# Another sequence of the same operations: linear attention and an MLP-mixer on one core

## The chip, the cores and the metric

The kernel runs on one core of a Trainium2 chip. The metric is the device time of one execution in microseconds (us). Five engines have queues of their own: TensorE (PE, matmuls), VectorE (DVE), ScalarE (ACT), GpSimd (POOL) and SyncE (SP, which here issues loads and stores). Each engine takes its instructions strictly in order, and an instruction waits on semaphores for what other engines or transfers must have done.

## The reference

Two blocks, joined by a reshape. The first is a recurrence over the sequence for each of 4 batches and 8 heads (48 wide, 768 steps); the second is an MLP-mixer on the result, first over tokens, then over channels.

```python
B, H, S, D = 4, 8, 768, 48
for t in range(S):
    cur = np.einsum('bhd,bhe->bhde', u[None] * k[t], v[t])
    y[t] = np.einsum('bhd,bhde->bhe', r[t], state + cur)
    state = w[t][:, :, :, None] * state + np.einsum('bhd,bhe->bhde', k[t], v[t])
x = y.transpose(0, 2, 1, 3).reshape(B, S, H * D)
h = np.maximum(x.transpose(0, 2, 1) @ w_tok1, 0) @ w_tok2
z = x + h.transpose(0, 2, 1)
out = z + np.maximum(z @ w_ch1, 0) @ w_ch2
```

w_tok1 is 768x256, w_tok2 256x768, w_ch1 384x1536, w_ch2 1536x384.

## The kernel before

**Attention units.** A batch's 768 tokens are three units of 256, so there are 12 units, 0 to 11 (batch = unit // 3). A unit has 4 chunks of 64 tokens. Its pieces carry names, and the change speaks only of these names; `0.gram` is the piece gram of unit 0. In the ORDER of the later units they are written 3/gram.

- DVE: ends (the scan of the decay w from the end of each chunk, line 435), begins (the scan from its start, line 443), keys and queries (k and r multiplied by these, lines 440 and 446), put and mask (products from PSUM into the matrix of a chunk, lines 458 and 327).
- ACT: own0 to own3 (k times u, line 331), copied0 and copied1 (turned keys out of PSUM, line 350), by1 to by3 (the state times the decay of a chunk, line 501; by0 for the first chunk of a later unit), seen (line 389 or 392), taken0 to taken2 (the output into x, line 407), and the range checks small and large (line 427), which only set a flag that is read at the kernel's end.
- PE: own (k times u against r, line 315), tokens (keys turned, line 345), gram (k against r, line 315), carry (k against v for the state, line 365), up1 to up3 (the state's step, line 508; in units 3 to 11 on DVE), before (r against the states, line 380) and after (the chunk's matrix against v, line 401).
- Loads on SP: k, r, v and w of a unit (k0 is k of unit 0; rk3 is both of unit 3 in four transfers). Lines 188, 201, 181.

Units 0 to 2 have rooms of their own; from unit 3 on k and r use two buffers in turn. For unit 0 to 2, own, gram and before take turns in two PSUM buffers, so each waits until what was made two pieces before has been read out.

**Weights.** The weights come as 64-bit words and are turned on chip into 32-bit floats, in chunks of 1024 columns: t0 to t2 for the token weights, c0 to c8 for the channel weights. A chunk has the steps load (SP, line 261), plus and minus (ACT, lines 264 and 267), lead, two, value and sum (DVE, lines 270, 273, 277, 281). The `sum` of the ORDER's chunks is called put there.

**Mixer.** Batch 0 is computed with plain 32-bit matmuls: h0 to h11 (line 947; h[2c + i] is token chunk c and half i), relu0 and relu1 of the two halves (line 950), back0 to back5 (line 958, with an add on DVE, line 960), turn (x turned, line 969, with a copy on ACT, line 971), up (line 993, or 989 in its last third) and down (line 1004). Batches 1 to 3 split each factor into two or three rounded parts and use three passes of a faster matmul: hidden (667), back (726), turn (741), ends and joint (772, 774, 779; the up-projection, with POOL and DVE forming its parts in lines 754 to 765), down (790 to 792). The third parts of the weights lie in DRAM and come through a ring of 10 slots (line 626). The attention of batch b + 1 is worked in between the mixer's matmuls of batch b.

**What sets the order.** Two lists written into the source. The first part (units 0 to 2, token weights, c0, the h pieces and back0) is one call of `strict` with the pieces in their order (lines 1094 to 1109). The rest (1181 pieces) is put together by `interleaved` from nine streams: each digit of ORDER names the stream whose next piece follows (0 the mixer, 1 to 3 and 8 its side streams and the weights, 4 to 6 the units modulo 3, 7 the loads of units). `strict` chains all instructions of an engine in the order of the list:

```python
for ins in block.instructions[done:]:
    if ins.engine in in_turn:
        if in_turn[ins.engine]:
            tc.add_manual_dep(ins, in_turn[ins.engine], no_sync, reason="order of issue")
        in_turn[ins.engine] = ins.name
```

This holds for PE, DVE, ACT and SP. `behind(gate, f)` in addition holds the first instruction of f until the piece `gate` has ended; it is used for loads. The six PSUM banks of the later stage are handed out in the order of the list too.

## Time and profile before

| | us |
|---|---|
| runs | 477.54, 477.70, 480.27 (median 477.7) |
| the profiled execution | 478.31 |
| its span | 476.5 |

| engine | busy us | share of the span | instructions |
|---|---|---|---|
| PE | 459.1 | 96% | 5322 |
| DVE | 344.6 | 72% | 495 |
| ACT | 265.8 | 56% | 606 |
| POOL | 54.2 | 11% | 58 |

Loads and stores moved 85.34 MB, 179 GB/s on average over the span. A row of a timeline reads: start, duration, engine, line, operation, output<-inputs, how many instructions are merged in it, and in brackets how long the engine stood before it and what released it. A row of the waits reads: who, line, whom it waited for, total us, how often, the longest. A row by windows reads: the stretch, its length, busy us (and instructions) of PE, of its weight loads, of DVE, ACT and POOL, then the granted clock, the busy share of the transfer engines and GB/s.

### The profile page before, as it was taken

How to read it: one execution, taken by the hardware profiler on the slowest of the kernel's cores; microseconds unless marked ns; L12 is line 12 of the kernel's file. 1: busy time of each engine (PE TensorE's matmuls, PEld its weight loads, DVE VectorE, ACT ScalarE, POOL GpSimd, SP SyncE). 2: the span in 40 equal slices, each digit the busy share in tenths (PEclk: the TensorE clock that was granted, in tenths of full speed). 3: DMA queues.
4: the chain of work that ended last, by engine and by line, in shares of the span. 5: the costliest groups of instructions: out<-in, count | busy, mean ns of one | idle time of the engine just before them, and what ended most of it. 6: DMA issues, size and time to landing. Idle time of an engine off the chain costs nothing.

```text
span 476.5 us, 12778 instructions
## 1 busy us (share of the span) xinstructions
PE 459.1 (96%) x5322; PEld 409.6 (86%) x5322; DVE 344.6 (72%) x495; ACT 265.8 (56%) x606; POOL 54.2 (11%) x58
## 2 busy tenths in 40 slices
PE   3899999999999999999999999999999999999996
PEld 2776588856797668999999999999999999999995
DVE  7998797679598877876897998685587885235341
ACT  6699876674678856453747385351837554134140
POOL 1000000000000001231302002130304003032130
PEclk9999999999999999999999999999999999999999
DMA  8865745573584556963888842754784513336331
GB/s 313 317 221 217 188 169 191 180 275 99 152 228 138 177 179 207 284 186 100 252 283 232 294 154 56 198 173 141 215 227 150 167 61 84 115 101 199 86 99 54
DMA packets 45055, 85.34 MB, mean 179 GB/s; under 512 B 4736, under 2 KB 37376, under 8 KB 44992
## 3 DMA queue, kind: packets, MB, share of 16 engines
q1 hardware_dynamic: 44704, 84.37, 56.3%
q8 instruction: 43, 0.70, 0.6%
q14 instruction: 20, 0.16, 0.1%
q10 hardware_dynamic: 288, 0.10, 0.1%
HBM read 72.65 MB, written 11.80 MB: 177 GB/s over the span
## 4 chain that ended last, share of the span: by engine, by line
PE 90%; ACT 4%; DVE 2%; DMA 2%; issue 1%; SPq 0%; DVEq 0%; ACTq 0%
PE bank L1004 10%; PE bank L772 8%; PE bank L779 8%; PE bank L774 8%; PE bank L790 8%; PE bank L792 8%; PE bank L791 8%; PE bank L993 7%; PE bank L667 3%; PE bank L989 3%; PE bank L726 3%; PE bank L315 2%; PE bank L401 2%; PE bank L380 2%; PE kv_ps L365 2%; PE bank L669 2%
## 5 line engine op out<-in xcount | busy, mean ns | idle before, releaser
L765 POOL TENSOR_TENSOR z_high<-z_high 128x384 fp32r<-128x384 f32 x48 | 52.9, 1107 | 406.7 <-DMA ring<-third 186.8
L754 ACT ACTIVATE z_high<-bank 128x384 fp32r<-128x384 f32 x48 | 23.5, 489 | 58.1 <-PE bank L779 57.7
L772 PE MATMUL bank<-x_forms,forms 128*128 128x384 f32 x216 | 50.3, 341 | 0.0
L779 PE MATMUL bank<-z_more,forms 128*128 128x384 f32 x216 | 50.1, 340 | 0.0
L774 PE MATMUL bank<-x_forms,ring 128*128 128x384 f32 x216 | 49.3, 337 | 0.0
L761 DVE SCALAR_TENSOR_TENSOR z_high<-bank,z_high 128x384 fp32r<-128x384 f32 x48 | 26.5, 554 | 31.4 <-ACT z_high L754 29.4
L1004 PE MATMUL bank<-wch,z 128*128 128x384 f32 x144 | 48.1, 488 | 0.0
L790 PE MATMUL bank<-forms,z_high 128*128 128x384 f32 x140 | 47.8, 342 | 0.0
L792 PE MATMUL bank<-forms,z_high 128*128 128x384 f32 x140 | 47.1, 337 | 0.0
L791 PE MATMUL bank<-ring,z_high 128*128 128x384 f32 x140 | 47.1, 337 | 0.0
L798 DVE SCALAR_TENSOR_TENSOR x<-bank,x 128x384 f32<-128x384 f32 x35 | 18.8, 553 | 39.0 <-PE bank L792 38.9
L1004 PEld LDWEIGHTS bank<-wch,z 128*128 128x128 f32 x144 | 26.8, 190 | 17.2
L501 ACT ACTIVATE before<-state,to_end 112x48 f32<-112x48 f32 x132 | 33.1, 324 | 13.0 <-DVE state L516 7.6
L779 PEld LDWEIGHTS bank<-z_more,forms 128*128 128x128 f32 x216 | 39.0, 188 | 0.1
L772 PEld LDWEIGHTS bank<-x_forms,forms 128*128 128x128 f32 x216 | 38.3, 188 | 0.5
L774 PEld LDWEIGHTS bank<-x_forms,ring 128*128 128x128 f32 x216 | 38.6, 188 | 0.0
L993 PE MATMUL bank<-xT,wch 128*128 128x256 f32 x144 | 32.0, 381 | 0.0
L993 PEld LDWEIGHTS bank<-xT,wch 128*128 128x128 f32 x144 | 27.0, 190 | 3.7
L757 ACT ACTIVATE z_high<-z_high 128x384 fp32r<-128x384 f32 x48 | 25.2, 525 | 3.5
L790 PEld LDWEIGHTS bank<-forms,z_high 128*128 128x128 f32 x140 | 26.3, 188 | 0.2
L791 PEld LDWEIGHTS bank<-ring,z_high 128*128 128x128 f32 x140 | 26.3, 188 | 0.0
L792 PEld LDWEIGHTS bank<-forms,z_high 128*128 128x128 f32 x140 | 26.3, 188 | 0.0
(243 smaller groups left out, 961.2 us busy)
## 6 DMA issues: line engine op xcount, KB each, us to landing
ring<-third SPq DMA_DIRECT2D x144, 192.0 KB, 3.4
raw<-in_words_ch_dram SPq DMA_DIRECT2D x8, 1023.8 KB, 4.8
rk<-in_rk_dram SPq DMA_DIRECT2D x36, 192.0 KB, 5.2
near<-in_near_dram SPq DMA_DIRECT2D x8, 768.0 KB, 5.0
w<-in_w_dram SPq DMA_DIRECT2D x10, 520.5 KB, 5.1
vt<-in_v_dram SPq DMA_DIRECT2D x12, 384.0 KB, 5.0
out_dram<-x SPq DMA_DIRECT2D x17, 192.0 KB, 2.8
third<-forms SPq DMA_DIRECT2D x12, 192.0 KB, 3.3
```

The costliest lines, as they stand in the source:

```text
L501: act.mul(t[:ROWS, a], state[bt, g][:ROWS, a], by_last(c, j)[:, a:a + 1])
L757: act.mul(z_form(jt, 2), z_form(jt, 0).bitcast(f32), 1.0 / BASE)
L761: dve.scalar_tensor_tensor(z_form(jt, 1), a, 0.0, z_form(jt, 0).bitcast(f32), op0=ALU.max, op1=ALU.subtract)
L765: pool.tensor_add(z_form(jt, 2), z_form(jt, 2).bitcast(f32), z_form(jt, 1).bitcast(f32))
L772: pe.matmul(a, up[m], xf(0)[:, m], start=m == 0, stop=False)
L774: pe.matmul(a, low[:, m], xf(1)[:, m], start=False, stop=False)
L779: pe.matmul(banks["a", jt], joint, xf(2)[:, m], start=False, stop=m == 2)
L790: pe.matmul(a, z[0], up, start=first, stop=False, skip_group_check=True)
L791: pe.matmul(a, z[1], held[bt, s, half, 1, jt], start=False, stop=False, skip_group_check=True)
L792: pe.matmul(a, z[2], joint, start=False, stop=last, skip_group_check=True)
L993: pe.matmul(ps, now["wch1"][:, jt // 4, m, ts(jt % 4, 128)], xT[:, m, ts(s, SEG)], start=(m == 0), stop=(m == DM // 128 - 1))
L1004: pe.matmul(ps, zs[s][:, jt, ts(n, 128)], now["wch2"][:, jt, :], start=(jt == 0), stop=(jt == NJ - 1))
```

## The change

No operation is added, removed or resized. The list of the first part is now a string of names, FIRST, in another order; ORDER has other digits. What a name stands for is as before; `a<b` holds a until b has ended, with the same gates as before. The two range checks of a unit are now two names, small and large.

```diff
--- before.py
+++ after.py
@@ -48,17 +48,28 @@
 SHRINK = (1.0 - 1.0 / BASE) ** 2
 LEAST, MOST = 2.0 ** -40, 2.0 ** 40
 MID = 3 * G // 4 * SEG1
+FIRST = (
+    "k0 masks 0.own0 0.own1 0.ends 0.own2 0.begins 0.own3 r0 0.large v0 k1 0.own 1.own0 1.own1 0.keys w1 0.queries 0.put 1.ends 1.own2 "
+    "0.tokens 1.own3 1.keys 0.copied0 1.begins 0.gram 0.mask r1 0.copied1 w2 0.small 0.carry 0.up0 0.by1 0.up1 0.by2 0.up2 0.by3 2.ends "
+    "t0.load<0.tokens 1.tokens t0.plus 1.copied0 1.copied1 1.own 1.queries 0.before 0.seen k2<1.ends 2.own0 v1<0.by2 2.own1 0.up3 1.by0 "
+    "0.after 1.put 1.carry 1.up0 2.own2 2.own3 r2<0.tokens 0.taken1 t0.minus 2.own 1.by1 1.up1 2.keys 2.tokens 0.taken0 t0.lead t0.two 1.by2 "
+    "1.up2 0.taken2 2.put 1.gram t1.load 1.by3 v2 t2.load<1.by1 1.up3 t0.value t0.sum 1.before 2.copied1 h1 2.copied0 1.mask t1.minus h3 "
+    "2.by0 2.carry 2.up0 1.seen 1.after 2.begins t1.plus 2.by1 2.up1 h0 1.taken1 2.queries 2.gram 1.taken0 2.by2 2.up2 1.taken2 h2 t1.lead "
+    "h5 2.by3 t2.plus 2.before h7 2.seen t1.two t2.minus 2.mask 2.after h4 2.taken0 2.taken1 t1.value t1.sum c0.load<1.gram h6 t2.lead "
+    "t2.two t2.value t2.sum 2.taken2 h8 c0.plus h9 c0.minus c0.lead c0.two h10 h11 relu1 c0.value relu0 back0 c1.load<2.own c2.load<1.tokens "
+    "1.large v3 rk3 w3<2.by3 2.large 1.small 2.small"
+)
 ORDER = (
-    "888008088078808800000888484440800840804080880808804844088488400448088408008888080080884808884040488844488888084840880880"
...
+    "408880880008088800008888444404008888888880000008880000848844444088808048488844400888880000880888884447444888444000888000"
...
 )
 
 
@@ -533,7 +544,7 @@
         def each(f, n):
             return [lambda m=m: f(m) for m in range(n)]
 
-        return dict(ranges=each(ranges, 2), ends=ends, keys=keys, begins=begins, queries=queries, own_u=each(own_u, A),
+        return dict(small=lambda: ranges(0), large=lambda: ranges(1), ends=ends, keys=keys, begins=begins, queries=queries, own_u=each(own_u, A),
                     own_gram=own_gram, copied=each(copied, UC), taken=each(taken, 3),
                     own_put=own_put, products=[lambda n=n: products(n) for n in range(3)], sums_put=sums_put,
                     tokens=tokens, gram=gram, mask=mask, carry=carry, before=before, seen=seen, after=after,
@@ -1037,7 +1048,7 @@
         loads = piece(lambda: load_rk(i + 1), "loads", ("Q", 8.0, last("before", "gram", "tokens")))
         ends = piece(e["ends"], "ends", ("DVE", 2.6, last("small", "large", "by3", "w")))
         keys = piece(e["keys"], "keys", ("DVE", 1.25, k("ends") + last("loads")))
-        small, large = (piece(e["ranges"][n], name, ("ACT", 1.4, k("ends"))) for n, name in enumerate(("small", "large")))
+        small, large = (piece(e[name], name, ("ACT", 1.4, k("ends"))) for name in ("small", "large"))
         begins = piece(e["begins"], "begins", ("DVE", 2.35, k("ends")))
         tokens = piece(e["tokens"], "tokens", ("PE", 0.9, k("keys") + last("carry"), "k0", "k1"))
         copied = [piece(e["copied"][n], f"copied{n}", ("ACT", 0.6, k("tokens")), ("free", f"k{n}")) for n in range(2)]
@@ -1085,28 +1096,24 @@
     raw_words.append(turned["xT"].rearrange("p m t -> p (m t)").bitcast(u32)[:, :4 * PIECE])
     to_tok = conversion(("wtok1", "wtok2"), words_tok, rooms=lambda n: ((0, 1, 3)[n], n % 2))
     to_ch = conversion(("wch1", "wch2"), words_ch, rooms=lambda n: (n % 2, n % 2) if n else (2, 2))
-    e0, e1, e2 = (unit(i) for i in range(UB))
-    (_, p0, n0, lead0, two0, put0, add0), (_, p1, n1, lead1, two1, put1, add1), (_, p2, n2, lead2, two2, put2, add2) = to_tok
-    _, p3, n3, lead3, two3, put3, _ = to_ch[0]
+    first = {i: unit(i) for i in range(UB)}
     in_turn.update({pe.engine: None, dve.engine: None, act.engine: None, sp.engine: None})
-    s0, s1, s2 = (e["updates"] for e in (e0, e1, e2))
-    t0, t1, t2 = (e["scaled"] for e in (e0, e1, e2))
-    strict(lambda: load_part(0, 1), masks, e0["ends"], e0["own_u"][0], e0["own_u"][1], e0["own_u"][2], e0["own_u"][3], e0["begins"],
-           lambda: load_part(0, 0), e0["keys"], lambda: load_part(1, 1), e0["own_gram"], lambda: load_v(0), e0["ranges"][0], lambda: load_w(1),
-           e0["tokens"], e0["queries"], e1["own_u"][0], e1["own_u"][1], e0["copied"][0], lambda: load_w(2), e0["gram"], e1["ends"], e0["copied"][1],
-           lambda: load_part(1, 0), e0["carry"], e1["own_u"][2], s0[0], e0["own_put"], e1["own_u"][3], e0["ranges"][1], t0[1], s0[1],
-           behind(e0["tokens"], to_tok[0][0]), e1["begins"], behind(e1["ends"], lambda: load_part(2, 1)), e1["own_gram"], t0[2], e1["keys"],
-           e2["own_u"][0], s0[2], e2["own_u"][1], e1["own_put"], t0[3], e1["tokens"], behind(e0["tokens"], lambda: load_part(2, 0)),
-           e0["before"], e2["own_u"][2], e0["mask"], e1["copied"][0], p0, e0["seen"], s0[3], e2["own_u"][3], behind(t0[2], lambda: load_v(1)),
-           e2["ends"], e1["copied"][1], t1[0], e0["after"], e0["taken"][0], e1["carry"], n0, to_tok[1][0], s1[0], e1["queries"], e0["taken"][1],
-           e2["keys"], lead0, t1[1], e2["own_gram"], two0, s1[1], e0["taken"][2], e2["own_put"], e2["tokens"], t1[2], put0, e2["copied"][0],
-           s1[2], t1[3], e2["copied"][1], e1["gram"], s1[3], e1["before"], t2[0], p1, add0, lambda: load_v(2), e1["mask"], e2["carry"], e1["seen"],
-           h[1], s2[0], h[0], e2["ranges"][0], e2["begins"], behind(t1[1], to_tok[2][0]), t2[1], n1, h[3], e2["queries"], s2[1], lead1, two1,
-           e1["after"], t2[2], s2[2], put1, e2["gram"], behind(e1["gram"], to_ch[0][0]), h[2], e1["taken"][0], e1["taken"][1], t2[3], e1["taken"][2],
-           behind(t2[3], lambda: load_w(3)), p2, add1, e2["mask"], lambda: load_v(UB), behind(e2["own_gram"], to_ch[1][0]), e2["before"], h[4],
-           e2["seen"], n2, e2["after"], lead2, two2, h[5], e2["taken"][0], h[6], e2["taken"][1], put2, e2["taken"][2], h[7], h[8], p3,
-           h[10], add2, n3, behind(e1["tokens"], to_ch[2][0]), lead3, two3, rectified[0], h[9], h[11], rectified[1], e1["ranges"][0], e2["ranges"][1], e1["ranges"][1],
-           lambda: load_rk(3), put3, lambda: turned["back"](0))
+    named = {"masks": masks, "rk3": lambda: load_rk(3), "back0": lambda: turned["back"](0)}
+    named.update({f"h{n}": f for n, f in enumerate(h)})
+    named.update({f"relu{n}": f for n, f in enumerate(rectified)})
+    for kind, weights in (("t", to_tok), ("c", to_ch[:3])):
+        for n, steps in enumerate(weights):
+            named.update({f"{kind}{n}.{name}": f for name, f in zip(("load", "plus", "minus", "lead", "two", "value", "sum"), steps)})
+    for i, e in first.items():
+        named.update({f"{'rk'[n]}{i}": lambda i=i, n=n: load_part(i, n) for n in range(2)})
+        named.update({f"w{i + 1}": lambda i=i: load_w(i + 1), f"v{i}": lambda i=i: load_v(i)})
+        for name, made in e.items():
+            name = {"own_u": "own", "own_gram": "own", "own_put": "put", "scaled": "by", "updates": "up"}.get(name, name)
+            named.update({f"{i}.{name}{n}": f for n, f in enumerate(made)} if isinstance(made, list) else {f"{i}.{name}": made})
+    named["v3"] = lambda: load_v(UB)
+    for name in FIRST.split():
+        name, _, gate = name.partition("<")
+        strict(behind(named[gate], named[name]) if gate else named[name])
 
     six_banks.close()
     ps_g, ps_m = None, six_banks.enter_context(tc.tile_pool(name="ps_m", bufs=1, space=bass.MemoryType.PSUM))
```

The old list of the first part and the new one, by engine and in the same names:

```
PE  old: 0.own 0.tokens 0.gram 0.carry 0.up0 0.up1 1.own 0.up2 1.tokens 0.before 0.up3 0.after 1.carry 1.up0 2.own 1.up1 2.tokens 1.up2 1.gram 1.up3 1.before 2.carry h1 2.up0 h0 h3 2.up1 1.after 2.up2 2.gram h2 2.before h4 2.after h5 h6 h7 h8 h10 h9 h11 back0
PE  new: 0.own 0.tokens 0.gram 0.carry 0.up0 0.up1 0.up2 1.tokens 1.own 0.before 0.up3 0.after 1.carry 1.up0 2.own 1.up1 2.tokens 1.up2 1.gram 1.up3 1.before h1 h3 2.carry 2.up0 1.after 2.up1 h0 2.gram 2.up2 h2 h5 2.before h7 2.after h4 h6 h8 h9 h10 h11 back0
ACT old: masks 0.own0 0.own1 0.own2 0.own3 0.small 1.own0 1.own1 0.copied0 0.copied1 1.own2 1.own3 0.large 0.by1 0.by2 2.own0 2.own1 0.by3 2.own2 1.copied0 t0.plus 0.seen 2.own3 1.copied1 1.by0 0.taken0 t0.minus 0.taken1 1.by1 0.taken2 1.by2 2.copied0 1.by3 2.copied1 2.by0 t1.plus 1.seen 2.small 2.by1 t1.minus 2.by2 1.taken0 1.taken1 2.by3 1.taken2 t2.plus 2.seen t2.minus 2.taken0 2.taken1 2.taken2 c0.plus c0.minus relu0 relu1 1.small 2.large 1.large
ACT new: masks 0.own0 0.own1 0.own2 0.own3 0.large 1.own0 1.own1 1.own2 1.own3 0.copied0 0.copied1 0.small 0.by1 0.by2 0.by3 t0.plus 1.copied0 1.copied1 0.seen 2.own0 2.own1 1.by0 2.own2 2.own3 0.taken1 t0.minus 1.by1 0.taken0 1.by2 0.taken2 1.by3 2.copied1 2.copied0 t1.minus 2.by0 1.seen t1.plus 2.by1 1.taken1 1.taken0 2.by2 1.taken2 2.by3 t2.plus 2.seen t2.minus 2.taken0 2.taken1 2.taken2 c0.plus c0.minus relu1 relu0 1.large 2.large 1.small 2.small
DVE old: 0.ends 0.begins 0.keys 0.queries 1.ends 0.put 1.begins 1.keys 1.put 0.mask 2.ends 1.queries 2.keys t0.lead t0.two 2.put t0.value t0.sum 1.mask 2.begins 2.queries t1.lead t1.two t1.value t1.sum 2.mask t2.lead t2.two t2.value t2.sum c0.lead c0.two c0.value
DVE new: 0.ends 0.begins 0.keys 0.queries 0.put 1.ends 1.keys 1.begins 0.mask 2.ends 1.queries 1.put 2.keys t0.lead t0.two 2.put t0.value t0.sum 1.mask 2.begins 2.queries t1.lead t1.two 2.mask t1.value t1.sum t2.lead t2.two t2.value t2.sum c0.lead c0.two c0.value
SP  old: k0 r0 k1 v0 w1 w2 r1 t0 k2 r2 v1 t1 v2 t2 c0 w3 v3 c1 c2 rk3
SP  new: k0 r0 v0 k1 w1 r1 w2 t0 k2 v1 r2 t1 v2 t2 c0 c1 c2 v3 rk3 w3
```

The ORDER's beginning, decoded: on ACT the old one starts with c1.plus c1.minus turn0 turn1 c2.plus c2.minus turn2 turn3 3/own0 to 3/own3, the new one with 3/own0 c1.plus c1.minus turn0 turn1 c2.plus turn2 turn3 c2.minus 3/own1 to 3/own3. On DVE the old one starts with c0.put back1 back2 c1.lead c1.two c1.value back3 c1.put back4 back5, the new one with back1 c0.put back2 c1.lead c1.two back3 c1.value back4 c1.put back5 (these back pieces are the adds of line 960). The loads of unit 4's k and r came first and now come behind the load of c8.

On PE the order of the mixer's own matmuls stays nearly as it was. The units' pieces stand between them in runs, each of them here in brackets with nothing else between:

```
old: [3/tokens] [3/own] [3/carry 3/gram] [4/tokens] [3/before 4/carry 4/gram 3/after] [5/tokens] [4/before 5/carry 5/gram 4/after] [5/before] [5/after] [6/tokens] [6/carry 6/gram] [7/tokens] [7/carry 6/before] [6/after 7/gram] [8/tokens] [7/before 8/carry] [8/gram 7/after] [8/before 8/after] [9/tokens] [9/carry 9/gram] [10/tokens] [9/before] [9/after 10/carry 10/gram] [11/tokens] [10/before] [11/carry 11/gram 10/after] [11/before 11/after]
new: [3/tokens 3/own] [3/carry 3/gram] [3/before] [4/tokens 3/after] [4/carry 4/gram] [4/before] [5/tokens] [5/carry 5/gram 4/after] [5/before] [5/after] [6/tokens] [6/carry] [6/gram] [6/before] [7/tokens 6/after] [7/carry 7/gram] [7/before] [8/tokens] [8/carry] [7/after 8/gram] [8/before] [8/after] [9/tokens] [9/carry 9/gram] [9/before] [10/tokens 9/after] [10/carry 10/gram] [11/tokens 10/before] [11/carry] [11/gram 10/after] [11/before 11/after]
```

More of the change, by code (lines that the diff above doesn't have):

```diff
@@ new lines @@
+FIRST = (
[9 rows of a table added]
+)
+ORDER = (
+    "408880880008088800008888444404008888888880000008880000848844444088808048488844400888880000880888884447444888444000888000"
+    "844000888888845500000008800008488588888440855885585544888800054808805555545558800700555558558888688500000008855050006666"
+    "666600888860088888876656688660066880666556099858886666888000066066666908988000990444444448800088444000884801110884440008"
+    "404428000000000000000000000000000202244440000700004444450000002204470000000050000000002000550005545500005452220004010100"
+    "155520555500000005550002455555000050500000000000000005500066600607066666060600566666666000006566660000006600000400000000"
+    "116660114100500001004400000222020516049916111166991110122110004432443322993442334444000070000010001100000444000000000000"
+    "000000000400044444000004555000000000000004005000000000000004440005054555050000000000145501000555510044005000070050000000"
+    "000555000055500055000000600660000000665500660000066600000000000000600000065566166616060000005611666616600102025562026669"
+    "111116660099010111122101032339922933000230000000001110000000000000000000000000000000000000000000000000000000000000000000"
+    "00000000000000010110000000000000000000000000000000000000700000000000000000000000000000000000000000000"
```

9 lines of the change are left out of this document (removed).

## The prediction

> **What bounds the kernel now.** I read the page's busy shares first, then the stretches by window, then the waits of TensorE.
>
> ```profile
> PE 459.1 (96%) x5322; PEld 409.6 (86%) x5322; DVE 344.6 (72%) x495; ACT 265.8 (56%) x606; POOL 54.2 (11%) x58
> ...
> 0.00:12.00 12.00, 3.71 (x76) 3.30 (x78) 9.01 (x14) 7.50 (x16) 1.26 (x10) 1.00 0.86 314
> 60.00:72.00 12.00, 12.00 (x62) 10.61 (x61) 11.72 (x15) 8.47 (x17) 0.00 (x0) 1.00 0.46 172
> 456.00:476.50 20.50, 15.79 (x91) 15.47 (x89) 6.16 (x12) 4.04 (x8) 3.91 (x4) 1.00 0.14 46
> ...
> PE gram L315 <- DMA rk<-in_rk_dram: 7.6, 1, 7.6
> PE kv_ps L508 <- ACT before L501: 1.4, 3, 1.0
> PE k_ps L345 <- issue: 0.7, 1, 0.7
> PE bank L969 <- ACT raw L267: 0.6, 1, 0.6
> PE bank L401 <- ACT seen L392: 0.6, 2, 0.3
> PE h_ps L947 <- issue: 0.5, 1, 0.5
> PE bank L401 <- issue: 0.5, 1, 0.5
> ```
>
> TensorE is busy 459.1 of 476.5 us. Of its 17.4 idle us, 7.6 are the wait for the first r rows, and 4.7 lie behind its last matmul (20.50 less 15.79); no reordering inside reaches either. The other waits in these rows, with the 0.42 in a row below, sum to 4.7. So the kernel has two stages: up to 60 us TensorE waits for ACT, DVE and the loads; from 60 us on its queue is full, and there a new sequence can only change what the switch from one kind of matmul to another costs, or open a new wait.
>
> **The start-up, to 24 us.** TensorE's rows, with one of ACT:
>
> ```profile
> 16.20 0.98 PE L508 MATMUL kv_ps<-before,ident 112*112 112x192 f32 x2 [0.99 <-ACT before L501]
> 17.11 1.99 PE L315 MATMUL gram<-rk,near 48*64 48x64 f32 x64
> 23.01 0.58 PE L508 MATMUL kv_ps<-before,ident 112*112 112x192 f32 x2
> 24.01 1.15 PE L401 MATMUL y_ps<-vt,at 64*64 64x48 f32 x64 [0.42 <-ACT seen L389]
> 30.53 1.16 PE L315 MATMUL gram<-rk 48*64 48x64 f32 x64
> ...
> 17.21 0.87 ACT L501 ACTIVATE before<-kv_ps,first 112x48 f32<-112x48 f32 x4 [1.07 <-PE kv_ps L508]
> ```
>
> Before, 0.up1 (16.20) is followed by 1.own (17.11), and 0.by2, which needs 0.up1, runs on ACT meanwhile (17.21). In the new order 0.up2 comes straight behind 0.up1 and needs that 0.by2: TensorE stands from about 17.2 to 18.1, 1.0 us. The same five pieces (up1, up2, 1.tokens, 1.own, 0.before) follow in either order, so 0.before ends 1.0 later. It is given back at 24.01: there 0.after waited for 0.seen, which stood on ACT behind t0.plus; now t0.plus follows 0.by3 at once: 0.up2 ends at 19.1, 0.by3 (0.87) at 20.1, t0.plus (1.2, the rows of ACT below) at 21.3, before 0.seen can run. I take 0; the ends are -0.5 (all of the wait and a little more) and +1.0 (nothing is given back). The new SP order (v0 ahead of k1, r1 ahead of w2, v1 ahead of r2) delays k1, w2 and r2 by one transfer each. I cost it at nothing, since TensorE's pieces at half rate from 10 to 16 us hide it; without that cover a transfer of 0.5 MB at the 314 GB/s of the first window is 1.7 us.
>
> The rows also show a clock that opens late: 64 matmuls of L315 take 1.99 us at 17.11 and 1.16 at 30.53, a pair of L508 0.98 at 16.20 and 0.58 at 23.01. The opening came about 6.8 us (23.01 less 16.20) after TensorE's last wait. The new last wait ends at 18.1. One row can't tell a delay after a wait from a fixed time, so the forecast moves nothing here, and rival 3 holds both ways.
>
> [...]
>
> **From 24 us to the first up-projection.** Rows of TensorE, ACT and DVE, two of DVE's at 38.59 and 41.00 for a rival:
>
> ```profile
> 43.62 1.24 PE L947 MATMUL h_ps<-x,wtok 128*128 128x384 f32 x3
> 45.38 3.81 PE L947 MATMUL h_ps<-x,wtok 128*128 128x384 f32 x11 [0.53 <-issue]
> 49.04 1.66 PE L958 MATMUL kv_ps<-h,wtok 128*128 128x384 f32 x4
> 59.08 3.19 PE L993 MATMUL bank<-xT,wch 128*128 128x256 f32 x14
> ...
> 6.12 1.70 ACT L331 ACTIVATE near<-rk,u_col 112x256 f32<-112x256 f32 x4 [1.54 <-DMA rk<-in_rk_dram]
> 43.76 1.45 ACT L407 COPY x<-y_ps 128x384 f32<-128x384 f32 x3 [0.64 <-PE y_ps L401]
> 47.95 0.49 ACT L950 ACTIVATE h<-h_ps 128x384 f32<-128x384 f32 x1 [0.36 <-PE h_ps L947]
> 49.62 1.16 ACT L427 ACTIVATE junk<-to_end,least 112x1041 uint8<-112x1041 f32 x1
> 50.90 1.17 ACT L427 ACTIVATE junk<-first,most 112x1041 uint8<-112x1041 f32 x1
> 54.46 1.21 ACT L267 ACTIVATE raw<-raw,rebias 128x1024 int16<-128x1024 int16 x1
> ...
> 38.59 1.29 DVE L277 SCALAR_TENSOR_TENSOR wtok<-raw 128x512 f32<-128x512 uint32 x2
> 41.00 1.30 DVE L327 COPY_PREDICATED at<-before_it,gram 128x1024 f32<-128x1024 uint8 x1
> 55.70 0.69 DVE L270 TENSOR_TENSOR raw<-raw 128x1024 int16<-128x1024 int16 x1 [1.83 <-ACT raw L267]
> 58.02 0.55 DVE L960 TENSOR_TENSOR x<-x,bank 128x384 f32<-128x384 f32 x1
> 58.49 1.22 DVE L281 TENSOR_TENSOR wch<-wch,raw 128x1024 f32<-128x1024 f32 x1
> ```
>
> 2.own2 and 2.own3 (0.43 each, the row at 6.12 has four) now stand on ACT between 1.by0 and 1.by1, and one taken copy less (0.48, a third of 1.45): 0.86 - 0.48 = 0.4 on the chain of by and up that leads through units 1 and 2. So unit 2's three taken copies end at 45.6 instead of 45.2 (43.76 + 1.45). But behind them TensorE has only h8 to h11 left, 8 passes instead of the 11 of the row at 45.38. At 0.33 us a pass (11 in 3.81, less the tail of the last) the last h ends at 45.6 + 0.1 + 2.6 = 48.3, where the old back0 began at 49.04; 0.5 later if the stand of 0.53 stays.
>
> Then 1) relu1 is queued ahead of relu0. back0 reads relu0's half first, and relu1 needs h11. So back0 starts after both: 48.3 + 0.1 + 0.4 + 0.5 = 49.3 instead of 49.04, where relu0 had run at 47.95. 2) On ACT four range checks (1.28 us apart, 49.62 to 50.90) stand there instead of three, since 2.small moved here, and 3/own0 (0.43) stands ahead of c1.plus: 49.2 + 5.1 + 0.4 = 54.7 for c1.plus, and c1.minus ends two times 1.15 later, at 57.0 (old 54.46 + 1.21 = 55.7). 3) On DVE lead, two and value follow (2.3, from 55.70 to 58.02), with the add of back3 queued between two and value and that of back4 behind value (0.5 each), then sum (1.2), 4.5 in all: c1 is ready at 61.6 (old 58.49 + 1.22 = 59.7). On TensorE turn3 waits for the add of back3 and the first up starts at about 59.2; 8 passes (1.7 us; the block at 59.08 has 14 in 3.19) bring it to 60.9, and there it waits 0.7 for c1. Old: 59.08 + 1.7 = 60.8 without a wait. **Term 1: +0.8**, ends +0.3 (if ACT gains half a microsecond) and +1.3 (if the issue stand stays).
>
> **From 62 us on.** The order of the large matmuls stays; what moves are the pieces of units 3 to 11, small 64-column matmuls, between them. The chain that ended last shows what a run of such pieces costs:
>
> ```profile
> 161.04 1.08 PE bank L380 x64
> 162.12 1.49 PE bank L669 x4
> 167.46 6.45 PE bank L669 x20
> 184.54 0.87 PE kv_ps L365 x64
> 185.40 0.95 PE bank L315 x64
> ```
>
> A large pass of L669 takes 0.32 (6.45 / 20). Behind a run, four of them take 1.49 instead of 1.29: leaving a run costs 0.20. Entering costs 0.13: a piece is 1.08 alone and 0.95 behind another. So each run beyond the tokens pieces (alike in either place) costs 0.33. Decoded, the old order has 18 such runs and the new 27: 9 x 0.33 = 3.0. In five of the new ones tokens stands first and may pay the entry, 5 x 0.13 = 0.65 less: 2.3. If a run begun by tokens paid nothing extra, 4 x 0.33 = 1.3. **Term 2: +2.6**, ends +1.3 and +3.0.
>
> Against this, 8.before and 8.after no longer stand side by side, so one of the two waits for seen (L392) goes, 0.3; and 8.gram with 7.after, where the 0.5 of issue fell, is split from 8.carry and 7.before. **Term 3: -0.8**, ends -1.1 (the other's share too) and 0 (the stand moves elsewhere).
>
> The producers of the moved pieces I followed by their place in the ACT and DVE queues, where the busy shares (72 and 56%) leave room: 3.by3, 4.keys and 4.by3 stand well ahead of 3.before, 4.tokens and 4.before, and the last form/0 steps two up passes ahead of their reader. I estimate 2 us of cover or more at each, and no new wait; where that cover is gone, TensorE stands for what is missing.
>
> **Sum.** 0.8 + 2.6 - 0.8 = +2.6 on the profiled execution's 478.3 (span 476.5 and 1.8 around it): 480.9. The median of the runs shown is 477.7, 0.6 under it: 480.3.
>
> **Rivals.** (1) *Nothing shows.* The issue stand goes, runs led by tokens are free, both waits go: 0.3 + 1.3 - 1.1 - 0.5 = 0: 477.7. For it: one order's switches are small against 477. Against: 0.33 at each run in the row. (2) *The k rows of unit 3 hold ACT*, the slow side. 3/own0 now stands at ACT's head at 54.3, ahead of c1 and the turn copies, and its rows are loaded behind c1 and c2.
>
> ```profile
> 41.76 11.99 SPq L188 DMA_DIRECT2D rk<-in_rk_dram x8
> rk<-in_rk_dram SPq DMA_DIRECT2D x8, 192.0 KB, 11.9
> ```
>
> These loads were issued from 41.76 and took 11.9 us. The load of c1 goes ahead of them and waits for t1.value, which ended at 39.9 (38.59 + 1.29) and now has 2.mask ahead of it (1.3) and the 0.4 from above: 41.6. With c1, c2 and v3 issued 0.45 apart the k rows go out at 43.0 and 43.5 and land at 54.9 and 55.4 if they take as long; each us past 54.3 is one more on TensorE, through c1.minus. Landing at 57.5 costs 3.2: 483.5; beyond 1% it decides from 56.5 on. Against: w3 no longer goes ahead of them. (3) *The clock*, both ways. Opening 3.4 us earlier runs 1.own and 0.before at full rate, 0.83 (1.99 less 1.16) and, with 48 of 64 passes, 0.6: 1.4, so 478.9; opening late, 0.after (1.15 to 2.0), 0.up3 (0.58 to 0.98) and half of 1.carry (0.4) slow down, 1.6: 481.9. (4) *Faster.* All 4.7 us of inner waits go, and the extra runs cost nothing: 473.0, or less with the clock.
>
> **How the numbers follow.** Forecast 0.46; rival 1 0.18; rival 2 0.18; rival 3 0.10, half each way; rival 4 0.08. 1% of 477.7 is 4.8 us, about what a measurement can tell from no change. Over 482.5 lie most of rival 2 and the upper part of the forecast and of the late clock: 0.26. Under 472.9: 0.06. Between: 0.68. Lower ends (0.3 + 1.3 - 1.1 - 0.5 - 1.4 of clock) give 476.3, and the upper (1.3 + 3.0 + 0 + 1.0 and 1.7 of late rows) 484.7; I widen the lower to 475.8.
>
> **What would show it.** TensorE's row of 0.up2 at about 18.1 with a wait for ACT; back0's first row at 49.3 behind ACT h; a wait of the third block of the first up (L993) for DVE wch; the last taken copy near 45.6; single small runs with 1.08 and the large passes behind them 0.20 over; no wait for seen at 8.after. Wrong if TensorE starts L993 before 59 or keeps it waiting past 63, or if stands over 1 us appear after 62 us.

## The result and the profile after

The new sequence is slower. Its median is 483.57 us (480.65 to 484.95) beside 478.37 us (477.25 to 480.28) of the kernel before on the same chip; the medians are 5.2 us apart. The ratio over all the runs of both is 1.0094, 95% interval 1.0072 to 1.0115, which makes +4.5 us, as do the spans of the two profiled executions; 4.5 is used below. Ratios leave out runs that fell into a slower state (one of e2, two of e4); the medians given do not. The profiled execution took 482.73 us, its span 481.0. The line numbers after the change are those of before plus 11; in the experiments they are plus 12.

The busy line of the page after the change, and then TensorE's waits:

```profile
PE 461.4 (96%) x5322; PEld 409.6 (85%) x5322; DVE 344.3 (72%) x495; ACT 266.4 (55%) x606; POOL 57.1 (12%) x58
```

```profile
PE gram L326 <- DMA rk<-in_rk_dram: 8.4, 1, 8.4
PE kv_ps L519 <- ACT before L512: 2.2, 3, 1.0
PE bank L980 <- DVE x L971: 1.4, 1, 1.4
PE kv_ps L969 <- ACT h L961: 1.0, 1, 1.0
PE bank L326 <- issue: 0.7, 1, 0.7
PE bank L1004 <- DVE wch L292: 0.4, 1, 0.4
PE bank L412 <- ACT seen L403: 0.3, 1, 0.3
```

Every engine has as many instructions as before. The waits on ACT and DVE that belong to the start have grown: 0.up and 1.up (L519) 2.2 instead of 1.4, turn3 (L980) 1.4 instead of 0.6, and back0 (L969), which stood 1.0. TensorE in order of time:

```profile
18.17 0.98 PE L519 MATMUL kv_ps<-before,ident 112*112 112x192 f32 x2 [0.96 <-ACT before L512]
24.00 1.15 PE L412 MATMUL y_ps<-vt,at 64*64 64x48 f32 x64
49.89 1.56 PE L969 MATMUL kv_ps<-h,wtok 128*128 128x384 f32 x4 [0.96 <-ACT h L961]
60.33 0.52 PE L980 MATMUL bank<-ident,x 128*128 128x128 f32 x3 [1.44 <-DVE x L971]
60.68 1.89 PE L1004 MATMUL bank<-xT,wch 128*128 128x256 f32 x8
62.97 3.29 PE L1004 MATMUL bank<-xT,wch 128*128 128x256 f32 x14 [0.40 <-DVE wch L292]
```

The third block of the first up (its ninth pass) is a good place to cut the span: there both kernels have left the start-up, and behind it TensorE is busy nearly all the time (from 60 us on 410.77 of 416.50 us before, 414.79 of 421.00 after). After, it starts at 62.97. Before, it started without a wait at 60.80 (59.08 and eight passes of 0.216). So of the 4.5 us of span (481.0 less 476.5) 2.2 lie ahead of the cut and 2.3 (418.05 instead of 415.69) behind it. The same cut serves for every experiment below: "start" is the time of that pass, "rest" what is left of the span.

ACT and DVE around it, which tell where the 2.2 us came from:

```profile
44.58 1.45 ACT L418 COPY x<-y_ps 128x384 f32<-128x384 f32 x3 [0.64 <-PE y_ps L412]
48.96 0.87 ACT L961 ACTIVATE h<-h_ps 128x384 f32<-128x384 f32 x2 [0.57 <-PE h_ps L958]
49.72 1.17 ACT L438 ACTIVATE junk<-to_end,most 112x1041 uint8<-112x1041 f32 x1
53.58 1.17 ACT L438 ACTIVATE junk<-first,least 112x1041 uint8<-112x1041 f32 x1
55.80 0.51 ACT L342 ACTIVATE near<-rk,u_col 112x256 f32<-112x256 f32 x1 [0.96 <-DMA rk<-in_rk_dram]
57.33 1.21 ACT L278 ACTIVATE raw<-raw,rebias 128x1024 int16<-128x1024 int16 x1
...
58.56 0.69 DVE L281 TENSOR_TENSOR raw<-raw 128x1024 int16<-128x1024 int16 x1 [3.57 <-ACT raw L278]
61.70 1.22 DVE L292 TENSOR_TENSOR wch<-wch,raw 128x1024 f32<-128x1024 f32 x1
```

Read downwards: both relu (L961), four range checks (L438), then ACT stands 0.96 for the k rows of unit 3, and 3/own0 (L342) and c1.plus and minus follow. c1.minus (L278) ends at 58.5 instead of 55.7 before, DVE has stood 3.57 for it, and c1 is ready at 62.9 (61.70 + 1.22), where TensorE waits for it.

### The profile page after: what moved, and what is told of

The parts are those of the page before. It is cut to its first block, busy times and chain, and to the rows that moved or that the text cites. A ratio compares the mean times of both kernels' runs of the same rounds, so it can differ in the third digit from the quotient of the medians.

```text
span 481.0 us, 12769 instructions
## 1 busy us (share of the span) xinstructions
PE 461.4 (96%) x5322; PEld 409.6 (85%) x5322; DVE 344.3 (72%) x495; ACT 266.4 (55%) x606; POOL 57.1 (12%) x58
## 4 chain that ended last, share of the span: by engine, by line
PE 91%; DMA 4%; ACT 2%; DVE 1%; issue 1%; SPq 1%; DVEq 0%; ACTq 0%
PE bank L1015 10%; PE bank L783 8%; PE bank L790 8%; PE bank L801 8%; PE bank L785 8%; PE bank L803 8%; PE bank L802 8%; PE bank L1004 6%; DMA rk<-in_rk_dram 4%; PE bank L678 3%; PE bank L1000 3%; PE bank L737 3%; PE bank L326 2%; PE kv_ps L376 2%; PE bank L391 2%; PE bank L412 2%
## 5 line engine op out<-in xcount | busy, mean ns | idle before, releaser
L776 POOL TENSOR_TENSOR z_high<-z_high 128x384 fp32r<-128x384 f32 x48 | 55.9, 1172 | 408.4 <-DVE z_high L772 213.5
L785 PE MATMUL bank<-x_forms,ring 128*128 128x384 f32 x216 | 49.3, 337 | 0.0
L1015 PE MATMUL bank<-wch,z 128*128 128x384 f32 x144 | 48.3, 489 | 0.0
L809 DVE SCALAR_TENSOR_TENSOR x<-bank,x 128x384 f32<-128x384 f32 x35 | 18.8, 552 | 36.3 <-PE bank L803 36.1
```

The source lines that it names most:

```text
L776: pool.tensor_add(z_form(jt, 2), z_form(jt, 2).bitcast(f32), z_form(jt, 1).bitcast(f32))
L785: pe.matmul(a, low[:, m], xf(1)[:, m], start=False, stop=False)
L1015: pe.matmul(ps, zs[s][:, jt, ts(n, 128)], now["wch2"][:, jt, :], start=(jt == 0), stop=(jt == NJ - 1))
```

## The experiments

### The two halves of the change

The kernel with the old FIRST and the new ORDER, and the one with the new FIRST and the old ORDER:

```
e1: FIRST = (the old list of pieces, as names);  ORDER = (digits of after)
e2: FIRST = (as after);                          ORDER = (digits of before)
```

> The old list of the first part with the new ORDER. Theory (start-up and switches add up, and the start-up loss is an interaction of both lists): the later stage pays its 2.4 us for 27 instead of 18 runs of small matmuls; in the start-up ACT has only three range checks ahead, but 3/own0 at its head waits for the k rows of unit 3, which the old load order lands at about 55, so c1 is ready at about 62.5 and TensorE's third up block starts 1.8 us later than before. Sum about +4.2 us on before. Rival A (all of the start-up loss sits in the first list): +2.4. Rival B (all of it sits in the new ORDER): +4.5 with the third up block at 63.

> The new list of the first part with the old ORDER. Theory: no extra runs, so nothing in the later stage; in the start-up relu1 ahead of relu0 costs back0 0.85 us and the fourth range check moves c1.plus to 54.9, but c1's sum is ready at 61.3, before TensorE comes to it at 61.7: +0.9 us on before. Rival A: +2.2, the whole start-up loss. Rival B: 0.

Measured: 482.4 us for the first, ratio 1.0084 [1.0062, 1.0107], +4.0 us (expected +4.2), with start 62.49 and rest 417.8; 479.2 for the second, ratio 1.0026 [1.0004, 1.0047], +1.2 us (expected +0.9), with start 62.34 and rest 415.3. So all of the +2.3 behind the cut is ORDER's. The start is lost by either half alone (1.7 and 1.5 us, together 2.2): ORDER puts 3/own0 ahead of c1.plus, FIRST turns the relus round and lets a fourth range check stand ahead of c1. In the first, ACT stood 0.85 for the k rows. By the clock record of its trace it also came to the full clock only at 30.0 us, where before and after did at 22.6, so a part of its 1.7 can be the clock's.

### More and fewer runs, in the kernel before

If each entry into and exit from a run of small matmuls costs 0.33 us, more runs must cost and fewer must pay. Only ORDER is changed:

```
e6: 18 runs split to 35, e.g. [3/before 4/carry 4/gram 3/after] -> [3/before] [4/carry] [4/gram] [3/after]
e5: 18 runs merged to 14, e.g. [7/before 8/carry] [8/gram 7/after] -> [7/before 8/carry 8/gram 7/after]; 9/tokens between 8/before and 8/after
```

> The kernel before with the runs of small matmuls taken apart: a large piece of the mixer is drawn between any two of them (35 runs instead of 18), all else as before. Theory of 0.33 us a run: 17 x 0.33 = 5.6 more, less the two waits for seen (1.0), which the large piece covers: 4.6 us over the kernel before, all of it after 62 us. Rival (the later stage of the kernel after was slower for other reasons than the number of runs): within 1 us of the kernel before.

> The kernel before (old first list, old ORDER) with five changes of place: 6.before between 7.carry and 7.gram with 6.after behind them, 7.before and 8.carry moved to 8.gram and 7.after, 9.before to 10.carry, 10.before to 11.carry (14 runs of small matmuls with a switch instead of 18), and 9.tokens put between 8.before and 8.after. Theory of 0.33 us a run: 4 x 0.33 = 1.3 less, and 0.5 less for the wait of 8.after for seen: 1.8 us under the kernel before, or 2.5 if the stand of 0.7 at TensorE's matmul 3272 goes as well. Rival (the switch cost is not paid by run, or PSUM banks and waits for seen take it back): no change, or slower.

Split: expected 4.6 over before, measured 486.4 us, ratio 1.0153 [1.0138, 1.0167], +7.4. Time between the large passes less that of the bare pieces rose from 7.78 to 12.38 us: 4.60 for 17 more runs, or 0.27 each; in it some 0.6 us of waits that went are counted against them. The miss of 2.8 is elsewhere. Most of it is in two new waits of the mixer's up for ACT, and the start was 0.5 later (61.33):

```profile
PE bank L1001 <- ACT x L419: 1.2, 1, 1.2
PE bank L1001 <- ACT z L1002: 0.6, 1, 0.6
```

Merged: expected faster by 1.8, measured 489.2, ratio 1.0217 [1.0198, 1.0235], +10.4. The small saving was there, and something larger came with it. Waits of TensorE, and the run [7/before 8/carry 8/gram 7/after]:

```profile
PE bank L413 <- issue: 4.4, 2, 3.0
PE bank L327 <- issue: 3.6, 2, 2.0
```

```profile
254.97 0.73 PE L413 MATMUL bank<-vt,at 64*64 64x48 f32 x36
258.68 1.09 PE L413 MATMUL bank<-vt,at 64*64 64x48 f32 x26 [2.98 <-issue]
```

Inside a run of four pieces TensorE stands up to 3 us for nothing that the profile names, and so, with 1.7 to 3.9 us over the price of a run, in each of the four runs so made (the two that had four pieces already have no such stand), and the 26 passes behind it go at half rate (1.09 instead of the 0.66 of the same passes before). In all there are 8.0 us of such stands behind the cut, and behind two of them the clock was withdrawn, for 6.8 and 3.4 us. My price for a run was about right and my idea that longer runs pay was wrong.

### The k rows of unit 3 earlier

ACT's 0.96 us for the k rows should go if they are loaded earlier. First far ahead (issued from 34.8 us on instead of 43.7), then two transfers ahead, between c1 and c2:

```
e3: ... c0.load<1.gram rk3 h6 ... back0 c1.load<2.own c2.load<1.tokens 1.large v3 w3<2.by3 ...
e7: ... back0 c1.load<2.own rk3 c2.load<1.tokens 1.large v3 w3<2.by3 ...
```

> The kernel after, with the loads of unit 3's k and r (rk3) moved on SP from behind v3 to straight behind c0's load, nothing else. Theory: they land before 42 us, ACT's wait of 0.96 us ahead of 3/own0 goes, c1 and TensorE's third up block come 1.0 us earlier, and the run is 1.0 us under the kernel after (about +3.5 on before). Rival: TensorE is held at turn3 by DVE's add anyway and the time does not move (+4.5).

> The kernel after with the four loads of unit 3's k and r between c1's and c2's load, not behind v3. Theory of the start-up: ACT's wait of 0.96 us for them goes and the third up block comes 1.0 us earlier: 1.0 us under the kernel after. Rival (what e3 showed: loads issued ahead of an instruction packet of TensorE make it late): a stand put down to issue of 1 us or more appears among the h pieces and the time goes up by as much, with the clock closing if it lasts over 2 us.

Far ahead: expected 1.0 better than the change, measured 488.5 us, ratio 1.0202 [1.0166, 1.0238], 5 us worse than the change itself, all of it in the start (69.64, rest 417.7). ACT's wait had gone, but TensorE, from 43 to 52 us and by the stretch from 48 to 60:

```profile
45.40 1.14 PE L392 MATMUL y_ps<-before,first 48*64 48x48 f32 x60 [1.24 <-issue]
48.38 0.59 PE L959 MATMUL h_ps<-x,wtok 128*128 128x384 f32 x1
51.46 5.20 PE L959 MATMUL h_ps<-x,wtok 128*128 128x384 f32 x11 [2.49 <-issue]
```

```profile
48.00:60.00 12.00, 8.55 (x52) 4.64 (x45) 6.37 (x8) 7.02 (x11) 0.00 (x0) 0.86 0.48 195
```

Two stands of the same nameless kind, and behind the second the granted clock of the stretch is 0.86: 11 passes take 5.20 instead of the 3.81 of before. Two transfers ahead: 481.1 us, ratio 1.0060 [1.0036, 1.0085], 1.6 us better than the change (expected 1.0), no new stand of over 0.7; but the start, 62.57, is only 0.4 earlier, since both relu ended 0.7 later than after the change and the full clock came at 28.9. With the k rows in time, the four range checks still hold c1 back.

### The start mended

To e3 and to e7 I added relu0 ahead of relu1 and 3/own0 behind the turn copies:

```
h8 c0.plus h10 c0.minus relu0 c0.lead c0.two h9 h11 relu1 c0.value back0;   in ORDER 3/own0 behind the copy of turn3
```

> As the run before, and in addition relu0 stands ahead of h9, h11 and relu1 (as in the old list), and 3/own0 stands behind the copies of turn2 and turn3 instead of at ACT's head. Theory: back0 starts at 49.0, c1.plus at 54.8 behind the four range checks, the third up block at 61.7: 1.3 us under the kernel after (about +3.2 on before), the rest of the start-up loss (0.8) staying with the fourth range check and DVE's order, and 2.4 in the later stage. Rival (the later stage gives the gain back or holds all of the loss): no change against the kernel after.

> As the run before, with relu0 ahead of h9, h11 and relu1 and 3/own0 behind the copies of turn2 and turn3. Theory of the start-up: back0 at 49.0, c1.plus at 54.8, the third up block at 61.7: 1.3 us under the kernel after, about +3.2 on before, the later stage keeping its 2.4. Rival (a late instruction packet): a stand of 1 us or more among the h pieces, and no gain.

Expected were 1.3 us under the change. On e3: 485.5 us, its runs from 480.0 to 489.4, ratio 1.0110 [1.0064, 1.0156], the stands as there (2.8 and 1.3 us) and one more of 1.2. On e7: 482.2, ratio 1.0069 [1.0046, 1.0092], start 61.94, rest 418.6. Over e7 the mending moved the start by 0.6, less than the medians can tell; over the change it is 1.0 of the 2.2 us.

### What the nameless stands are

TensorE's instructions are brought by transfers: the page of the kernel before has, in its table of queues, 43 packets with 0.70 MB, 16 KB each. They are TensorE's: with 26 or 64 further matmuls at its head and nothing else (below) there are 44, 0.72 MB, and in every other queue as many as before.

```profile
q8 instruction: 43, 0.70, 0.6%
```

Counting TensorE's passes through the traces, the stands put down to issue lie before passes 858 and 985 (e3), 2892, 3272, 4158 and 4540 (e5) and 3272 (before and after): always close to a multiple of 127 apart (divided by 127 they leave 94 to 98). 127 passes with their 127 weight loads are 254 instructions. Not every stand of this kind lies there: the 0.7 us of the kernel before at pass 64 (L345, 10.28 us) and one of 1.0 us at 19.4 us with the longer head below do not, and they are not explained.

A packet starts about one ahead of the one in use: that of the stand before pass 3272 at pass 3168, 104 passes ahead in the kernel before.

The first sight of it came from another question, the clock of the start (rival 3). 26 matmuls of the identity were put at TensorE's head, where it stands for the first r rows:

```python
filled = bank("warm")
for _ in range(26):
    pe.matmul(filled[:, :128], ident, ident, start=True, stop=True)
```

> The kernel before, and 26 further matmuls of the 128x128 identity against itself (result unused) as TensorE's first work, from about 1.6 us on, where it stood until 7.6 waiting for the first r rows. This prices the clock, rival 3 of the prediction. If the opening follows TensorE's work (a stretch of busy time and then the full rate), it opens between 5 and 9 us instead of at 22.6; the pieces from 7.6 to 22.6, at half rate in the kernel before, then halve from 14.5 to about 8 us, but ACT, DVE and the loads of k1 and r1 take over as bounds: back0 1.5 to 4 us earlier than 49.04 and the whole 1 to 3 us under before. The rival: the opening has its own time or closes again in the stands that follow, then the whole is within 1 us of before. A third way: the wave of small issue stands is the true bound of the start, then nothing moves either though the clock is open.

> The kernel after with the same 26 matmuls at its head. If the clock costs the start, as much is gained as in the kernel before (1 to 3 us on after); the difference of +2.2 us between the two starts, which I put on ACT's queue (k rows, range checks, relu order), stays. If instead the difference between the starts comes from the clock (rival 3), it shrinks to under 1 us.

496.9 us in the kernel before (ratio 1.0386 [1.0350, 1.0421]) and 488.9 in the one after (1.0207 [1.0177, 1.0238]). The clock did open: the first gram, 64 passes in 1.98 us otherwise, took 1.16. But the head took 8.9 us, not the 6 that were free, and the clock was withdrawn again, in the first kernel from 17.7 to 28.0 us. Neither start gained (62.94 and 67.78, with two stands of 1.6 and 2.2 us put down to issue in the second), so these runs do not settle rival 3. In the kernel before, 17.3 us were lost behind the cut (rest 433.0), 120 to 380 us away from the head, where 10.7 us of issue stands lie instead of 0.5. The head:

```profile
1.53 8.90 PE L1119 MATMUL warm<-ident 128*128 128x128 f32 x52 [1.53 <-POOL ident masks.py:199]
10.37 1.16 PE L327 MATMUL gram<-rk,near 48*64 48x64 f32 x64
```

The theory then: TensorE's stream is cut into packets of 16 KB, each is fetched only about one packet ahead (104 passes in that case), and a stand comes where a packet's border falls into small matmuls that use up 127 passes faster than the next packet arrives. What is put at the head moves all borders against the work. So a head of one packet (64 small matmuls, 128 passes with their weight loads, beside the 127 counted) must leave everything in place, and a shorter one must not:

```python
filled, made = [bank("shift") for q in range(2)], []
for _ in range(64 // 4 + 1):        # the shorter head: 26 in place of 64
    fours(lambda q, j, rows, cols: len(made) < 64 and made.append(pe.matmul(
        filled[q][cols, :16], ident[rows, :T], ident[rows, :16], start=True, stop=True)))
```

> The kernel before, with 64 further small matmuls (128 passes of 16 columns and 128 weight loads, result unused) as TensorE's first work while it stands for the first r rows; everything behind them is the same. In the traces so far TensorE's instructions come in packets of about 16 KB, and every stand of over 0.6 us put down to issue lies at a multiple of 127 passes of the stream (731, 858, 985, 1748, 2130, 2892, 3272, 4158, 4286, 4540, 4667). 256 added instructions are one packet, so the packets' borders fall on the same work as in the kernel before. Theory (packets): the stand stays in 8.gram with 7.after, the stretch behind the first up keeps its 415.7 +- 1 us, and the whole is within 1.5 us of before (the head itself may cost up to 1 us where it delays the first gram). Rival (whatever is put ahead delays, or a clock that opens otherwise): it goes as the kernel with 26 matmuls of the identity at its head, which took 18 us more, 17 of them behind the first up.

> The kernel before with 26 of the same small matmuls at its head (52 passes and 52 weight loads, 0.4 of a packet): shorter than the 64 of the other kernel, but the packets' borders fall on other work, the same as in the kernel with 26 matmuls of the identity. Theory (packets): the stands of that kernel come back at the same passes (731, 1748, 2130, 3272, 4286, 4667 of the stream), each 1 to 4 us, and the whole is 10 to 18 us over before, though fewer instructions were added than in the other kernel. Rival: the loss of that kernel came from its 9 us at the head and the clock it opened; then this one is within 2 us of before.

The longer head, one packet: 478.56 us beside 478.63, ratio 1.0005 [0.9988, 1.0023], start 61.00, rest 415.55; its stand behind the cut lies before the same 26 passes of 7/after. The shorter one: 494.3 us, ratio 1.0357 [1.0313, 1.0401], +15.6 by the medians and +17.1 by the ratio, start 62.23, rest 429.6. Behind the head both run the same 5322 passes in the same order; the longer head costs nothing and the shorter one some 16 us, as expected of both. The rival falls: the shorter head ends at 3.2 us, and TensorE then waits for the first rows as before.

The kernel with the shorter head: TensorE's waits, the ends of two runs in its timeline, [3/before 4/carry 4/gram 3/after] and [11/carry 11/gram 10/after], and the clock by stretches.

```profile
PE bank L413 <- issue: 7.6, 3, 3.4
...
PE bank L784 <- issue: 1.0, 1, 1.0
```

```profile
126.91 0.87 PE L413 MATMUL bank<-vt,at 64*64 64x48 f32 x45
129.78 0.55 PE L413 MATMUL bank<-vt,at 64*64 64x48 f32 x18 [2.00 <-issue]
130.25 4.22 PE L1016 MATMUL bank<-wch,z 128*128 128x384 f32 x7
...
377.92 1.12 PE L413 MATMUL bank<-vt,at 64*64 64x48 f32 x62
382.43 0.20 PE L413 MATMUL bank<-vt,at 64*64 64x48 f32 x1 [3.39 <-issue]
```

```profile
120.00:140.00 20.00, 18.00 (x307) 13.52 (x306) 11.03 (x14) 10.31 (x26) 0.00 (x0) 0.91 0.59 154
...
157.00:170.00 13.00, 10.82 (x129) 6.84 (x119) 11.06 (x15) 8.81 (x21) 0.00 (x0) 0.87 0.76 222
...
378.00:400.00 22.00, 18.33 (x277) 17.66 (x266) 15.23 (x26) 11.34 (x31) 0.00 (x0) 0.92 0.47 151
```

Behind the cut there are 8.6 us of such stands (7.6 and 1.0), where the kernel before has 0.5. After the three long ones the clock is withdrawn for a while: seven passes of L1016 take 4.22 us instead of some 2.3 at 0.32 each, and the three stretches show a mean clock of 0.91, 0.87 and 0.92. Summed over the large passes this is another 4.7 us: 12.8 of the 13.9 by which the rest grew. The stands of over 1 us lie before passes 731, 1748, 2130, 4286 and 4667 of the stream, five of the six expected; at 3272 none is left. The two at 1748 and 2130 are in the two runs of four pieces that had no stand before, and the longest, at 4667, is in a run of three. Single packets can be seen in the transfer view. The first row is that of the 0.1 us from 253.4 on in the kernel before, the second that from 380.2 on in this one:

```profile
q8 instruction: 1, 0.02, 80.7%
```

```profile
q8 instruction: 1, 0.02, 58.2%
```

The first starts 104 passes ahead of its border and is used from 256.2 on, 2.8 us later, when the stand of 0.5 ends. The second starts when TensorE has stood for it since 379.0 (377.92 and 1.12), and is used from 382.4 on, 2.2 us later. 64 small passes take about 1 us, so a packet full of them is used up in some 2 us, less than the next one takes to come. The second one also started late. For the stands of e3 the record shows why: its only edit against the change is the place of the four loads. After the change a packet starts at 36.58 us, at pass 735; in e3 none starts between 35.3 and 42.58, at pass 851, seven passes ahead of the first stand. The stretch between, first in e3 and then after the change:

```profile
36.58:42.58 6.00, 6.00 (x188) 4.47 (x187) 4.39 (x5) 4.49 (x15) 0.00 (x0) 1.00 1.01 266
```

```profile
36.58:42.58 6.00, 6.00 (x199) 4.45 (x191) 4.42 (x7) 4.98 (x16) 0.00 (x0) 1.00 0.05 14
```

With the loads issued from 34.8 us on the transfer engines are full (1.01), where they had almost nothing to do (0.05), and the packet follows the one before it by 7.3 us instead of 3.7. In the kernel with the shorter head, too, their share was 0.80 from 376.3 to 380.2, ahead of the late packet; but no run took those transfers away, and there it stays likely.

One more comparison falls out. The shift by 52 passes costs the old order 13.9 us behind the cut (this head) or 17.3 (the 26 larger matmuls), the new order 1.1 (419.13 instead of 418.05), with one stand of 1.7 us, in its run of three pieces [5/carry 5/gram 4/after]; 4.8 more were lost in its start. The new order has one run of three pieces; the old one has two of four and two of three. At this one shift the new order is far less exposed behind the cut; other shifts were not tried.

## Why the prediction held in direction and was too small

The forecast was +2.6 us (480.3); measured were +4.5 by the ratio. The median lies in the range, at the time of rival 2 (483.5). That is luck: rival 2 reached it by a wait of 3.2 us that measured 0.96, and 0.7 of it is only that the kernel before measured 478.4 and not 477.7. One sign of being wrong was missed by a hair: TensorE was kept waiting to 62.97, where 63 was named.

**Start to 24 us: 0.** As forecast: 0.up2 at 18.17 (18.1) behind a wait of 0.96 for ACT, 0.after at 24.00 (24.01 before) with no wait left. In part this is luck too: the first r rows came 0.8 later (8.36 instead of 7.59), and the issue stand of 0.7 behind the first gram was gone, so 0.tokens began at 10.28 in both.

**Term 1: +0.8, measured +2.2; this step failed.** It named each link rightly and made most too short. Unit 2's taken copies ended at 46.0 (forecast 45.6), the last h at 48.9 (48.3; its last twelve passes ran without a break from 44.4) and the last relu at 49.8 (49.3), so 0.5 was missing before c1's turn came. Then ACT stood 0.96 for the k rows, and that is rival 2's mechanism, at less than a third of its price. I had put their landing at 54.9 and 55.4 for an ACT that wants them at 54.3; it wanted them at 54.84 and had them at 55.80. My own rows thus gave a wait of 0.6 to 1.1, and that belonged in the sum, not among the rivals. So c1.minus ended at 58.5 and not at 57.0, and the third block began at 62.97 and not at 61.6. Loading the k rows earlier (e7) and changing the order on ACT as well (e8) bring it to 62.57 and 61.94. The 1.1 us left over 60.80 are not taken apart.

**Term 2: +2.6, by count 3.0, its upper end.** Open was whether a run led by tokens pays for its entry. It does, by the chain that ended last, after the change:

```profile
112.79 5.16 PE bank L1015 x16
...
119.02 1.49 PE bank L1015 x4
120.51 0.77 PE bank L356 x8
121.28 1.08 PE bank L412 x64
122.35 6.65 PE bank L1015 x20
```

16 large passes take 5.16, 0.3225 each. Behind tokens (L356), 3/after (L412) takes 1.08 and not 0.95, and the 20 passes behind it 6.65 instead of 6.45: 0.13 and 0.20, as with any other run. Nine more runs are 9 x 0.33 = 3.0. e6 priced 17 more at 4.60, 0.27 each, which would make 2.4; so the size holds to some 0.06 us a run.

The price falls due where the small tiles meet passes of 128x128 (1.08 for a piece alone, 1.49 instead of 1.29 for the four large passes behind one), not between two small pieces (0.95).

**Term 3: -0.8, measured -0.4; its second half failed.** The wait for seen went from 8.after, and 0.5 us with it rather than 0.3. The issue stand did not go. TensorE after the change, in the run [7/after 8/gram]:

```profile
256.57 1.15 PE L412 MATMUL bank<-vt,at 64*64 64x48 f32 x64
257.54 0.89 PE L326 MATMUL bank<-rk 48*64 48x64 f32 x47
259.08 0.46 PE L326 MATMUL bank<-rk 48*64 48x64 f32 x17 [0.66 <-issue]
```

Before, it stood in [8/gram 7/after], in 7/after with 26 passes to go; now in 8/gram with 17 to go. In both kernels this is before pass 3272 of TensorE's stream. I had taken a packet's border for a property of the pieces that stood there.

**Sum behind the cut.** 3.0 - 0.4 makes 2.6, where 2.4 were measured (418.05 less 415.69). **Rival 1** is out, since runs led by tokens pay and the stand stays, and so is **rival 4**. **Rival 3:** by the clock records of their traces both profiled executions came to the full rate at 22.6 us, so the clock is no part of the difference between them. In the other profiles here those records show it at 20.8 to 36.3, in six of them after 3.4 or 6.8 us of full rate from 14 or 15 us on that were withdrawn again. My prices for it were also too high: with the longer head the full rate came at 29.0, and the first row of back0 at 49.22 instead of 49.04.

With the shorter head the clock was withdrawn from 130.6 to 134.0, from 161.3 to 164.7 and from 383.2 to 386.6, 3.4 us each time; in the last of them the large passes follow at 0.32 us, ahead of it and behind it at 0.17. What decides when it opens or closes no run shows. The 6.8 us after the last wait were chance in one row; after the change they were 4.4 (18.17 to 22.61). That the clock might open 3.4 us earlier, on which rival 3's early side and the 1.4 of clock in my lower end stand, was an assumption that no row of the kernel before showed; stretches of that length are in the traces named here, but the two kernels compared opened within 0.01 us of each other (22.60 and 22.61).

## What to carry to other kernels

TensorE's instructions are loads too: in these traces some 127 passes with their weight loads are one 16 KB packet, and a stretch of small matmuls uses it up (64 passes in about 1 us, so a packet in some 2) faster than the next one comes (2.8 and 2.2 us from its start to its use); so break long stretches of small matmuls with large ones, against a price of some 0.3 us a break (as here), and count the passes ahead of a stand that the profile puts down to issue. How short is short enough depends on where the borders fall: runs of four and of three pieces showed stands of 1.4 to 3.7 us in some kernels and none in others, one run of two showed 1.6 (at 3272, with the 26 matmuls of the identity), and e6, with two runs of two and the other pieces apart, none behind the cut, though it was 7.4 us slower in all. Matmuls added ahead shifted all later borders here (26 short ones made 8.6 us of stands behind the cut out of 0.5); before an edit is credited with a gain or a loss, see whether it moved them, and pad to a whole packet to tell. And a wait that one's own rows already show belongs in the sum, not among the rivals.

## What the hardware showed that I had not expected

52 short passes at the head of the kernel before cost 15.6 us, and 128 of them nothing. The three stands of 2.0 to 3.4 us behind the shorter head were paid a second time, since large passes behind each ran at half rate for some 3.4 us (4.7 us in all). And loading rows earlier cost 5 us on TensorE, which was not waiting for them, because its instructions came late (7.3 us behind the packet before them instead of 3.7). None of the twelve variants is faster than the kernel before; the one with the padded head equals it.
